# Attention and channel mix in one hand-ordered kernel: a new order of steps, filler matmuls ahead of the first sums, and two store queues for the last four tiles

## The chip, the cores and the metric

The kernel runs on one core of one Trainium2 chip. The metric is the device time of one execution, in microseconds. The core has TensorE (PE, with its weight loads listed as PEld), VectorE (DVE), ScalarE (ACT), GpSimd (POOL) and SyncE (SP). Each of them takes its own instructions strictly in the order of the program, apart from weight loads, which can be fetched ahead. ACT, POOL and SP also issue transfers.

## The reference, cut to what matters

There are 8 batches, 8 heads, 576 positions and 64 elements per head; `phi` has 32 memory slots per head.

```python
a = exp(phi - max(phi)); a = a / (sum(a) + 1e-9)
k_m = einsum('bhsm,bhsd->bhmd', a, k);  v_m = einsum('bhsm,bhsd->bhmd', a, v)
scores = q @ k_m.T / sqrt(64);  attn = softmax(scores)
x = (attn @ v_m), heads side by side: (8, 576, 512)
x_prev = x moved down by one position, zeros in front
xk = mu_k * x + (1 - mu_k) * x_prev;   xr = mu_r * x + (1 - mu_r) * x_prev
k2 = relu(xk @ w_k) ** 2               # 512 -> 1024
out = sigmoid(xr @ w_r) * (k2 @ w_v)   # (8, 576, 512)
```

## The kernel before, in words

**The order of the work.** Everything after the set-up is a list of short words, `PLAN` (lines 19 to 57). Lines 674 to 687 walk through it: the first time that a word such as `1:s` comes, the step starts and issues its instructions up to its first `yield`; the next time, it goes on from there. So `1:s 1:s 1:s` is the score matmuls of batch 1, then the exponentials of its first half of heads, then those of the second half. Words between two such parts are issued between them. Since each engine works in the order of issue, `PLAN` is the order of every engine's queue. `BANKS` (line 60) gives, in order of creation, which of the 8 PSUM banks each matmul result takes.

**The words.** `p:` words issue loads on POOL's queue (`preload`, line 165): `p:k:1` is k of batch 1, `p:wk:0-4` the first half of `w_k`'s columns. The loads of k, v, q and the weights turn f32 into bf16 on the way. k and v of a batch share one of two buffers, and so do q and phi, so batch 3 follows batch 1 in the same place. A word with a batch number is a step of that batch's attention:

- `exp` (L255, ACT) makes the exponentials of phi; `z` (L289, PE, and L293, DVE) sums them and takes the reciprocal `rz`; `kv`, `k`, `v`, `kg`, `vg` (L279, PE) are the sums over positions; `c00d` and the like (L262 ACT, L264 DVE) cast k of batch 0, which ACT's queue loads in f32 as `k0f`.
- `ak`, `nk` (L315 ACT, L317 DVE) scale `k_m` by `rz`; `tk` (L345 PE, L351 DVE) transposes it; `q0`, `q1` (L364, DVE) turn q; `s` (L377 PE, L385 ACT) gives scores and their exponentials `e`.
- The softmax sums of batches 1 to 7 are made on DVE: `fe` (L411), `fs` (L417, L418), `fo` (L423), then `w0`, `w1` (L430). For batch 0 they are made by PE and ACT: `l` (L393 PE, logarithm L401 ACT), `hNz` or `rNz` (L406 ACT, exp of the negative logarithm; `h` is one half of the positions of one half of the heads, `r` all positions), then `y` or `w` (L430 DVE).
- `x0`, `x1` (L336 PE, L444) are attention times values in two halves of the positions, copied out by ACT; `xv` gives half of the copies to DVE. `dd` (L456) takes the difference to the position before; `k0d`, `r2e` and the like (L467 or L469, then L471) make xk and xr: `d` scales on DVE, `e` on ACT, and DVE adds. Batch 0 has mixed weights instead: `mk`, `mr` (L336, `mxps`, PE) and `uk`, `ur` (L517; `a` on ACT, `d` on DVE).

Words with `c` are the first matrix of the channel mix: `c3:1s` is columns 128 to 255 of `w_k` for the fourth stretch of tokens (L603, PE), then relu and square. Without a letter the relu is on ACT (L611) and the square on DVE (L620); with `s` both are on ACT (L618); with `v` both are on DVE (L609, L620). Stretch 0 is batch 0 and has two halves, `a` of 320 and `b` of 256 positions; the later stretches are 512 tokens, the last 448. `g:5` (L636 PE, L640 ACT) is the gate of 128-token tile 5, `o:5` (L653 PE, L659 DVE) its second matrix and the product, followed by `store` (lines 579 to 591). The last tile, 35, is done in two parts of 384 and 128 columns.

**Filler.** `keep_busy` (line 215) issues matmuls on a tile of zeros whose result nobody reads (L219). `WARM` issues 78 of 64 columns at the start; `0:busy7_2` issues 7 of 512 columns, `0:busy1x4_5b` one of 4 x 64.

**The table.** `0:tb` (L252) loads ACT's second table of functions; the first holds the logarithm that batch 0 needs.

**The store.** A tile of 128 tokens goes out in two pieces of 64 rows:

```python
            eng.dma_start(out=dst, in_=o[p:p + n, cols])
            if t >= NTOK // 128 - 2:
                eng = nc.scalar
```

so the first piece is issued by SP, and for tiles 34 and 35 the second by ACT; for all others both by SP.

Of the kernel before, what the change touches and what calls it, by code (L numbers as in the profile page):

```python
# [16 lines left out]


PLAN = [
# [37 lines left out]
]  # L57

WARM = (78, 1)
BANKS = (  # L60
    "0123456701452370614523670145276301452763014263015762310476251642510764235174236501423601754214215672"
    "4165704136257413605237415327605247610524761052467354263452741023745102637405127405127651402751402635"
    "4026154026351407435071570267135426071354607132456071345601256013427501345041245142572431546417452046"
    "054720413207512"
)

PRE = "q:0g id:"
# [9 lines left out]
def kernel(  # L77
# [18 lines left out]
    NTOK = B * S  # L96
# [482 lines left out]
    def store(o, t, cols):  # L579
        g = t * 128  # L580
        eng = nc.sync
        while g < (t + 1) * 128:
            b, r = divmod(g, S)
            p = g - t * 128
            j, p0 = divmod(r, QR)
            n = min(QR - p0, (t + 1) * 128 - g)
            dst = out[b].rearrange("(p j) d -> p j d", j=NJ)[p0:p0 + n, j, cols]
            eng.dma_start(out=dst, in_=o[p:p + n, cols])
            if t >= NTOK // 128 - 2:
                eng = nc.scalar  # L590
            g += n

# [50 lines left out]
    def value(t, hs=((0, 1),), n=1):  # L643

        def go():
            p = t * 128 % (2 * S)
            for n_, (h0, h1) in enumerate(hs):
                if n_:
                    yield
                cols = slice(h0 * Dm // n, h1 * Dm // n)  # L650
                pv = ps_tile([128, Dm], F32, "pv")
                for fi in range(NF):
                    nc.tensor.matmul(pv[:, cols], lhsT=sq[:, fi, p:p + 128],  # L653
                                     rhs=wv_sb[:, fi, cols], start=(fi == 0), stop=(fi == NF - 1))
                yield
                if t not in outs:
                    outs[t] = work.tile([128, Dm], F32, name="o", tag="o", bufs=4)
                o = outs[t]
                nc.vector.scalar_tensor_tensor(o[:, cols], in0=gated[t][:, cols], scalar=1.0, in1=pv[:, cols],  # L659
                                               op0=AL.add, op1=AL.mult)  # L660
                store(o, t, cols)
        return go
# [55 lines left out]
```

## Time and profile before

| what | us |
|---|---|
| median of 3 runs | 203.02 |
| the runs | 202.95, 203.02, 203.92 |
| the profiled execution, its own time | 203.86 |
| its span, first to last instruction | 202.1 |
| what lies around the span | 1.76 |
| PE busy (94% of the span) | 190.5 |
| DVE busy (74%) | 149.8 |
| ACT busy (69%) | 139.6 |
| mean clock granted to PE, share of full speed | 0.983 |

A row of a timeline is start, duration, engine, line, operation, result<-operands, count, and in brackets how long the engine stood idle before it and what ended that. A row of grouped lines is line, engine, operation, shapes, count, busy time, mean duration of one in ns, then idle time before. A row of windows is the stretch, its length, busy time and count of PE, PEld, DVE, ACT and POOL, the granted clock, the busy share of the DMA engines (it can pass 1) and GB/s. The load rows give bytes and microseconds from issue to landing.

### The profile page before, as it was taken

To read this page: it belongs to the slowest core of one execution; us is meant where nothing else is said; L and a number is where in the kernel's file an instruction comes from. 1 tells how busy PE (TensorE), PEld (TensorE's weight loads), DVE (VectorE), ACT (ScalarE), POOL (GpSimd) and SP (SyncE) were. 2 spreads that over 40 slices of the span, in tenths; PEclk is the share of its full clock that TensorE was granted. 3 is DMA by queue.
4 is the path that set the end of the run, shared out by engine and by line. 5 is a ranking of instruction groups with operands and counts; after the bars stand their busy time and mean duration, and the time that the engine had idled before them with its cause. 6 is when DMAs were issued, how large, how long until landed. Compare 5 with 4: busy or idle time off the path is not lost.

```text
span 202.1 us, 5328 instructions
## 1 busy us (share of the span) xinstructions
PE 190.5 (94%) x2171; PEld 100.0 (49%) x2192; DVE 149.8 (74%) x314; ACT 139.6 (69%) x310; POOL 28.5 (14%) x43
## 2 busy tenths in 40 slices
PE   7399999999999999999999999999999999999990
PEld 7235665675554445444447854444444444444450
DVE  2136789889999999999998998999983804735241
ACT  2428668977887999997979989884486591446030
POOL 7544210511005400027000000000000000000000
PEclk9759999999999999999999999999999999999999
DMA  5999999999999999669999700122512200342455
GB/s 192 278 208 266 206 207 257 209 224 238 258 278 249 233 284 213 205 152 232 212 225 229 193 2 13 43 55 52 133 24 54 57 0 20 84 103 56 104 133 128
DMA packets 24521, 31.88 MB, mean 158 GB/s; under 512 B 1960, under 2 KB 19120, under 8 KB 24496
## 3 DMA queue, kind: packets, MB, share of 16 engines
q0 software_dynamic: 16848, 20.32, 53.2%
q1 hardware_dynamic: 6336, 9.18, 18.0%
q10 hardware_dynamic: 1312, 2.03, 3.0%
q8 instruction: 17, 0.28, 0.5%
q14 instruction: 8, 0.07, 0.1%
HBM read 38.28 MB, written 9.44 MB: 236 GB/s over the span
## 4 chain that ended last, share of the span: by engine, by line
PE 78%; DMA 11%; DVE 5%; ACT 2%; issue 1%; POOL 0%; ACTq 0%; DVEq 0%
PE pk L603 28%; PE pv L653 24%; PE pr L636 13%; DMA kv<-in_v_dram 8%; PE kvps L279 4%; PE idle L219 3%; DMA k0f<-in_k_dram 3%; PE scps L377 2%; PE nops L336 1%; DVE diff L456 1%; DVE xkT L471 1%; PE zps L289 1%; DVE se L417 1%; PE mxps L336 1%; PE ktps L345 1%
## 5 line engine op out<-in xcount | busy, mean ns | idle before, releaser
L603 PE MATMUL pk<-xkT,wk 128*128 128x512 bf16 (+4 forms) x342 | 68.1, 339 | 1.3 <-DVE xkT L471 0.3
L653 PE MATMUL pv<-wv,sq 128*128 128x512 bf16 (+3 forms) x322 | 66.4, 353 | 0.3
L603 PEld LDWEIGHTS <-wk 128*128 128x128 bf16 x352 | 32.8, 98 | 29.2 <-issue 2.5
L611 ACT ACTIVATE rl<-pk 128x512 bf16<-128x512 f32 (+3 forms) x63 | 34.8, 568 | 16.5 <-PE pk L603 8.6
L653 PEld LDWEIGHTS <-sq 128*128 128x128 bf16 x328 | 30.8, 98 | 29.7 <-ACT sq L618 0.4
L659 DVE SCALAR_TENSOR_TENSOR o<-sg,pv 128x512 f32<-128x512 f32 (+3 forms) x41 | 24.4, 612 | 22.9 <-PE pv L653 12.4
L636 PE MATMUL pr<-wr,xrT 128*128 128x512 bf16 x139 | 34.9, 379 | 0.3
L640 ACT ACTIVATE sg<-pr 128x512 f32<-128x512 f32 x36 | 21.2, 606 | 15.1 <-DVE o L659 7.6
L618 ACT ACTIVATE sq<-rl 128x512 bf16<-128x512 bf16 (+5 forms) x56 | 26.0, 502 | 0.7
L636 PEld LDWEIGHTS <-xrT 128*128 128x128 bf16 x144 | 13.8, 98 | 16.1 <-DVE xrT L471 0.3
L467 ACT ACTIVATE mu_d<-diff,mu 128x576 bf16<-128x576 bf16 x24 | 17.1, 771 | 4.0 <-DVE diff L457 3.7
L444 ACT CAST x<-nops 128x256 bf16<-128x256 f32 (+1 forms) x46 | 15.6, 435 | 5.1 <-PE nops L336 4.9
L620 DVE TENSOR_TENSOR sq<-rl 128x512 bf16<-128x512 bf16 (+5 forms) x48 | 14.7, 334 | 3.5 <-ACT rl L611 3.1
L430 DVE TENSOR_TENSOR atn<-e,lz 128x576 bf16<-128x576 bf16 (+2 forms) x18 | 11.8, 687 | 1.3 <-ACT lz L406 1.1
L219 PE MATMUL idle<-zeros 128*128 128x64 bf16 (+3 forms) x103 | 11.5, 282 | 1.0 <-DVE zeros L150 1.0
L609 DVE TENSOR_SCALAR rl<-pk 128x512 bf16<-128x512 f32 (+3 forms) x17 | 9.8, 580 | 3.5 <-PE pk L603 2.2
L364 DVE STREAM_TRANSPOSE qT<-q 128x576 uint32<-128x576 uint32 x16 | 11.9, 760 | 0.2 <-DMA q<-in_q_dram 0.2
L385 ACT ACTIVATE e<-scps 128x288 bf16<-128x288 f32 x32 | 10.5, 417 | 2.2 <-PE scps L377 2.2
L471 DVE TENSOR_TENSOR xrT<-x,mu_d 128x1152 bf16<-128x1152 bf16 x14 | 10.5, 749 | 1.0 <-ACT mu_d L467 0.9
L456 DVE TENSOR_TENSOR diff<-x 128x1024 bf16<-128x1024 bf16 (+1 forms) x21 | 10.4, 552 | 0.8 <-ACT x L444 0.4
L469 DVE TENSOR_SCALAR mu_d<-diff,mu 128x576 bf16<-128x576 bf16 x32 | 10.8, 378 | 0.3
L255 ACT ACTIVATE em<-ph 128x1152 bf16<-128x1152 f32 (+1 forms) x9 | 9.6, 1069 | 1.8 <-DMA ph<-in_phi_dram 1.8
(68 smaller groups left out, 150.8 us busy)
## 6 DMA issues: line engine op xcount, KB each, us to landing
out_dram<-o SPq DMA_DIRECT2D x61, 128.0 KB, 2.4
ph<-in_phi_dram POOLq DMA_DIRECT2D x7, 576.0 KB, 16.4
kv<-in_k_dram POOLq DMA_DIRECT2D x7, 576.0 KB, 16.8
q<-in_q_dram POOLq DMA_DIRECT2D x7, 576.0 KB, 17.6
kv<-in_v_dram POOLq DMA_DIRECT2D x7, 576.0 KB, 15.6
k0f<-in_k_dram ACTq DMA_DIRECT2D x2, 576.0 KB, 6.8
wk<-in_moe_w_k_dram POOLq DMA_DIRECT2D x2, 512.0 KB, 13.8
wv<-in_moe_w_v_dram POOLq DMA_DIRECT2D x2, 512.0 KB, 20.2
```

Of the source, the lines that this page charges most:

```text
L219: nc.tensor.matmul(ps.rearrange("p (a b) -> p a b", b=64), lhsT=zeros, rhs=zeros[:, :64].unsqueeze(1).to_broadcast([128, blocks, 64]), sta ...
L444: (nc.vector.tensor_copy if both and i > 1 else nc.scalar.copy)(st["x"][:, i, sl], pss[i])
L467: nc.scalar.activation(t[:, i], st["d"][:, pr + i, :], AF.Copy, scale=mu1[:, o:o + 1])
L471: nc.vector.tensor_add(dst, st["x"][:, pr:pr + n], t)
L603: nc.tensor.matmul(pk[:, p0 - lo:p1 - lo], lhsT=wk_sb[:, di, fi * 128:(fi + 1) * 128], rhs=xk_T[:, di, p0 % RING:p0 % RING + p1 - p0], sta ...
L611: nc.scalar.activation(rl, pk, AF.Relu, scale=HALF ** 0.5)
L618: nc.scalar.activation(sq[:, fi, p:p + p1 - p0], rl[:, part], AF.Square)
L620: nc.vector.tensor_mul(sq[:, fi, p:p + p1 - p0], rl[:, part], rl[:, part])
L636: nc.tensor.matmul(pr, lhsT=xr_T[:, di, c0:c0 + 128], rhs=wr_sb[:, di, :], start=(di == 0), stop=(di == ND - 1))
L640: nc.scalar.activation(gated[t], pr, AF.Tanh, scale=0.5)
L653: nc.tensor.matmul(pv[:, cols], lhsT=sq[:, fi, p:p + 128], rhs=wv_sb[:, fi, cols], start=(fi == 0), stop=(fi == NF - 1))
L659: nc.vector.scalar_tensor_tensor(o[:, cols], in0=gated[t][:, cols], scalar=1.0, in1=pv[:, cols], op0=AL.add, op1=AL.mult)
```

## The change

1. The list of steps is a new one. It has the same attention steps, matmuls, loads and stores; some steps change the engine of their copies, scalings, relus and squares. In batch 0 two of the four reciprocals and weighings are merged: `0:h0z 0:h1z 0:y0 0:y1` become `0:r0z 0:w0`.
2. At the head, after the 78 fillers, one filler of 256 and 13 of 512 columns are put in before the first `0:z`; the other fillers of the head are distributed differently, and three single ones come later (`0:busy1_5`, `0:busy1x5_3b`, `0:busy1x3_1b`). The second cast on DVE (`c10d`) and the turn of q (`0:q0`) now come before the reciprocal of `0:z`. The table load `0:tb` moves from the middle of stretch 0 to the place between `0:uk0d` and `0:uk0a`.
3. POOL's loads are in another order: `wk:4-8`, `wk:0-4`, `phi:1` instead of `wk:0-4`, `phi:1`, `wk:4-8`; then k1, q1, wr, v1, wv, phi2, wv, v2, k2, q2 as before; then q3, k3, phi3, v3 instead of v3, phi3, k3, q3; then phi4, phi5, q4, k4, v4, k5, v5, q5, phi7, v6, phi6, k6, q6, k7, v7, q7 instead of phi4, k4, v5, v4, phi5, q4, q5, k5, phi7, k7, phi6, v6, k6, q7, v7, q6.
4. For the last four tiles, not two, the second piece is issued by ACT.
5. `BANKS` is another string to match.

The head and the end of the list, the line with the sums of batch 3 (`3:kv`), the stretch from the scores of batch 7 to its last word that makes xk, and the store:

```diff
 PLAN = [
-    "p:q:0h 0:exp1 0:c00d 0:c01a 0:exp0 0:z 0:kg0 0:busy7_2 0:z 0:c11a 0:c10d 0:kg1 0:q0 0:busy1x3_1b 0:ak 0:tk",
-    "0:busy1x4_5b p:v:0g 0:q1 0:busy1x4_2b p:v:0h 0:busy1x5_3b 0:busy1x4_4b 0:tk 0:s1 0:s1 0:s0 0:s0 0:mub 0:mub",
-    "0:busy2_1 0:l2 0:l2 0:l3 0:l3 0:busy3_5 0:h3z 0:y3 0:h2z 0:y2 0:l0 0:l0 0:vg0 0:l1 0:l1 0:h1z 0:vg1 0:nm1",
-    "0:busy5_0 0:nm0 0:y1 0:h0z 0:y0 0:busy2_3 0:busy1_4 0:mk1 0:uk1d 0:uk1a p:wk:0-4 0:mk0 0:uk0a c0:2b 0:uk0d",
-    "c0:1av c0:1av c0:1av c0:2av p:phi:1 1:exp 0:mr0 0:ur0a 0:ur0d c0:2b c0:2b c0:3bv c0:1bv 0:mu c0:2av c0:2av 0:mu",
-    "c0:1bv p:wk:4-8 1:z c0:6av c0:7as c0:7as c0:5bv p:k:1 1:k 1:z 1:ak c0:6av c0:6av c0:7as c0:3bv c0:0bs c0:4bv",
...
-    "g:5 o:7 2:fe 2:fs 2:fo 2:w0 g:7 2:w1 2:xv0 o:7 3:z 3:z 2:xv0 2:xv0 3:kv 2:xv1 2:xv1 p:phi:4 o:4 p:k:4 3:ak 2:xv1",
...
-    "c5:7 6:fs 6:fo 6:w0 6:w1 g:18 g:18 5:r2e o:18 o:18 c5:4s c5:4s c5:4s 7:s 7:s 7:s 7:fe 5:r2e 7:fs g:19 g:21 g:21",
-    "c5:7 g:19 7:fo 7:w1 c5:1 c5:1 c5:1 6:x0 6:x0 7:w0 o:17 c5:3s o:17 6:x0 6:x1 6:x1 6:x1 6:dd 6:k2d 6:k2d o:19 g:20",
-    "g:20 g:26 o:20 o:20 6:k0d 7:x0 o:19 7:x0 7:x0 g:26 g:22 o:21 o:21 6:k0d g:24 7:x1 g:22 7:x1 7:x1 7:dd 7:k2d",
-    "7:k2d 7:k0e o:23 7:k0e c6:2s c6:0s c6:0s c6:0s g:23 g:23 c6:6v 6:r0d c6:1s 6:r0d c6:7v c6:7v 6:r2e 6:r2e c6:6v",
...
-    "c8:7s o:32 o:34 o:34 g:32 o:32 o:28 g:35 g:35 o:28 o:33 g:33 o:33 o:35 o:35 o:35 o:35",
+    "0:exp1 0:busy1x4_2b 0:busy13_9 0:c00d 0:c01a 0:c10d 0:exp0 0:z 0:kg0 0:c11a 0:q0 0:z p:q:0h 0:busy7_2 0:kg1",
+    "0:busy2_e0 0:busy1x4_e0b 0:q1 0:ak 0:tk 0:tk 0:busy1x6_5b 0:busy1x7_e1b 0:s0 0:s0 0:s1 0:s1 0:busy1x4_4b",
+    "0:busy1_4 0:mub 0:mub 0:l0 0:l0 0:l1 p:v:0g 0:vg0 0:l1 0:r0z 0:l3 0:l2 0:l2 0:h2z 0:w0 p:v:0h 0:vg1 0:nm1",
+    "0:busy2_3 0:nm0 0:y2 0:l3 0:h3z 0:y3 0:busy2_1 0:busy5_0 0:mk0 0:uk0d 0:tb 0:busy1_5 0:mk1 0:uk1d 0:uk0a 0:uk1a",
+    "p:wk:4-8 c0:7as c0:7as 0:mr0 0:ur0d p:wk:0-4 c0:4bv c0:4bv 0:ur0a 0:mr1 c0:1bv c0:1bv c0:1bv p:phi:1 c0:2bv",
+    "c0:7as c0:7bv c0:7bv c0:7bv 1:exp 0:ur1d c0:2a c0:2a p:k:1 1:z c0:4as c0:4as c0:4as c0:0as c0:0as c0:0as 1:k",
+    "p:q:1 0:busy1x5_3b c0:4bv c0:2a c0:5bs 1:z 0:busy1x3_1b 0:ur1a 1:nk 0:mu 1:tk 1:tk 1:q0 1:q1 c0:5bs c0:5bs",
...
+    "2:x1 2:x1 g:4 3:q0 o:5 g:4 3:z 2:xv0 2:xv0 o:7 p:v:3 3:kv 3:z 3:av 3:ak o:4 2:xv0 2:dd 2:k2e 2:k0d 3:tk 3:tk o:6",
...
+    "c5:0s o:16 c5:2 7:tk 4:r2e 7:s c5:4s 7:s 7:s 5:r2d c5:7s c5:7s c5:0s c5:6 6:fs 6:fo c5:0s o:17 o:17 o:19 4:r2e",
+    "g:18 g:18 g:21 7:fe g:21 5:r2d g:23 o:16 g:23 c5:3s c5:3s g:19 g:19 6:w0 6:w1 6:x0 c5:2 6:x0 6:x0 o:18 7:fs",
+    "c5:3s 7:fo 6:x1 7:w0 o:18 6:x1 7:w1 g:20 6:x1 6:dd o:21 o:21 g:22 g:20 g:22 7:xv1 7:xv1 7:xv1 6:k0d 6:k0d 6:k2d",
+    "6:k2d o:20 7:x0 7:x0 7:x0 7:dd o:20 o:22 o:19 c6:0 c6:5 c6:5 c6:5 c6:0 c6:1 7:k0d 7:k0d c6:0 g:26 g:26 c6:1 o:23",
+    "7:k2d 7:k2d c6:4v c6:2s c6:2s c6:2s o:22 c6:4v c6:4v 6:r0d c6:1 c7:6s c7:6s g:25 c6:7s 7:r0d 7:r0d c8:2 c6:7s",
...
+    "c8:6 c8:6 c8:6 c8:7v c8:7v c7:3 c7:3 c7:3 g:35 g:34 g:34 c8:1v o:30 c8:4 c8:4 o:28 g:28 g:28 o:28 g:30 g:30 o:30",
+    "o:31 o:31 c8:5 g:33 g:32 c8:4 c8:5 o:29 o:33 o:32 o:29 g:32 o:32 o:33 g:35 o:34 o:34 o:35 o:35 o:35 o:35",
 ]
...
-            if t >= NTOK // 128 - 2:
+            if t >= NTOK // 128 - 4:
                 eng = nc.scalar
```

More of the change, by code (lines that the diff above doesn't have):

```diff
@@ L60 @@
 BANKS = (
[L61 to L64, printed above, removed]
+    "0123456701263470521653247061507642314057623140576237234523724571043752643756142376145037615024374370"
+    "1431762401362457016253401672351406725406732540673254163720432701643706125437061543706154320761543015"
+    "4632154601546512670354267034127534120354703546713254671325671432546371546325016472506725075235210451"
+    "2674132764374635270"
 )
```

47 rows, old and new, of the table PLAN are left out of this document.

## The prediction

> **What bounds the kernel now.** I read the page first: busy shares and the granted clock by slices of 5 us.
>
> ```profile
> PE 190.5 (94%) x2171; PEld 100.0 (49%) x2192; DVE 149.8 (74%) x314; ACT 139.6 (69%) x310; POOL 28.5 (14%) x43
> PE   7399999999999999999999999999999999999990
> PEclk9759999999999999999999999999999999999999
> ```
>
> PE is busy nearly all the time, so the end moves only if PE starts its real work earlier, runs it faster, or the tail after the last matmul shrinks. All that is missing of PE and of its clock lies in the first three slices and the last. Windows of a fraction of a microsecond give the clock's edges (columns: length, busy PE, PEld, DVE, ACT, POOL, clock, DMA share, GB/s):
>
> ```profile
> 4.40:5.00 0.60, 0.42 (x15) 0.30 (x11) 0.00 (x0) 0.00 (x0) 0.60 (x2) 1.00 1.08 421
> 7.25:7.50 0.25, 0.00 (x0) 0.00 (x0) 0.13 (x1) 0.25 (x2) 0.25 (x1) 0.99 1.11 295
> 7.50:7.75 0.25, 0.00 (x0) 0.00 (x0) 0.00 (x0) 0.25 (x2) 0.24 (x1) 0.50 1.09 290
> 14.20:14.40 0.20, 0.20 (x3) 0.14 (x2) 0.17 (x1) 0.00 (x0) 0.00 (x0) 0.70 1.29 215
> ```
>
> The column of the clock has 1.00 from the start, but the matmuls tell more: 15 of the 78 fillers fit into 0.42 us at 4.4, where all 78 took 3.83, so full speed began at about 4.1. The clock falls to half at 7.50 and is back at about 14.3. The timeline shows what PE did around that:
>
> ```profile
> 0.99 3.83 PE L219 MATMUL idle<-zeros 128*128 128x64 bf16 x78 [0.99 <-DVE zeros L150]
> 6.92 0.67 ACT L262 CAST kv<-k0f 128x576 bf16<-128x576 f32 x1 [0.88 <-DMA k0f<-in_k_dram]
> 7.50 0.68 ACT L255 ACTIVATE em<-ph 128x576 bf16<-128x576 f32 x1
> 8.23 0.40 PE L289 MATMUL zps<-ones,em 128*128 128x2 bf16 x9 [3.41 <-ACT em L255]
> 9.16 3.17 PE L219 MATMUL idle<-zeros 128*128 128x512 bf16 x7
> 9.83 0.46 DVE L264 CAST kv<-k0f 128x576 bf16<-128x576 f32 x1 [0.99 <-DMA k0f<-in_k_dram]
> 9.83 0.67 ACT L262 CAST kv<-k0f 128x576 bf16<-128x576 f32 x1 [1.65 <-DMA k0f<-in_k_dram]
> 10.20 0.77 DVE L364 STREAM_TRANSPOSE qT<-q 128x576 uint32<-128x576 uint32 x1
> 12.26 0.67 PE L279 MATMUL kvps<-kv,em 64*32 64x64 bf16 x36
> 12.97 0.62 ACT L315 ACTIVATE kbd<-kvps,rz 128x128 bf16<-128x128 f32 x2 [2.47 <-PE kvps L279]
> 20.07 0.70 PE L336 MATMUL mxps<-atn,vmm 32*64 32x256 bf16 x40
> 22.95 0.48 PE L336 MATMUL mxps<-atn,vmm 32*64 32x320 bf16 x24
> ```
>
> PE idles 3.4 us for the exponentials, then fills with 7 matmuls at 0.45 us each. The second half of k was cast at 10.50, but its sum starts only at 12.26: the slow fillers stand in front. Everything of batch 0 follows from there, up to 20.07. At full clock a 512-column matmul costs 1.73 / 8 = 0.216 us (chain of waits):
>
> ```profile
> 163.37 1.73 PE pv L653 x8
> ```
>
> **The change part by part.**
>
> *Filler, clock and the head.* The new fillers start at 4.82 and last 0.11 + 13 x 0.216 = 2.9 us, to 7.7; a gap of 0.5 us is left, for ACT still casts k ahead of the second exponentials, so the sum of phi stays at 8.23. The clock fell after 2.7 us without matmuls; I take it that 0.5 us doesn't do it. Then 9 + 36 small matmuls and 7 fillers (1.51) end by 10.4, and the sum of k starts when its cast is done, at 10.55: **1.7 earlier**. The reciprocal now stands behind the second cast and the turn of q on DVE: 9.83 + 0.46 + 0.77 + 0.16 = 11.23, later than the sum's end at 11.0, so the scaling of k starts at 11.28 instead of 12.97 (1.69 earlier). Transposes and scores at full clock give back another 0.3 to 0.4. ACT's softmax chain then has the same length within 0.1 (two half reciprocals become one whole). So the mixing matmuls start at about 17.9 instead of 20.07.
>
> There ACT now loads its table first. It cost
>
> ```profile
> 33.40 1.28 ACT L252 ACT_TABLE_LOAD   x1
> ```
>
> in the middle of stretch 0, where PE hid it. Now ACT is free at 17.4, loads until 18.7 and casts until 19.6 the two blocks that the first key needs; without the load it would cast from 18.3. Price 0.4. The first key ends at 19.9 with `mr0` next. Before, `mr0` started at 22.95 with three keys done; the changed kernel is at that point after two more keys (0.99): 20.9. Less two fillers in later words (0.13 + 0.08): **1.9 us** at equal work.
>
> *Loads.* They don't move with PE. POOL's queue moves the same first loads, and each takes what it took:
>
> ```profile
> 9.86 0.75 POOL L140 DMA_DIRECT2D q<-in_q_dram  x1 [2.12 <-DMA q<-in_q_dram]
> q<-in_q_dram POOLq DMA_DIRECT2D x1, 576.0 KB, 17.6
> 30.29 0.92 PE L377 MATMUL scps<-qT,kmT 32*32 32x288 bf16 x32
> 37.92 0.77 POOL L140 DMA_DIRECT2D q<-in_q_dram  x1
> q<-in_q_dram POOLq DMA_DIRECT2D x1, 576.0 KB, 22.9
> 41.80 0.76 POOL L136 DMA_DIRECT2D ph<-in_phi_dram  x1 [3.11 <-ACT em L255]
> ph<-in_phi_dram POOLq DMA_DIRECT2D x1, 576.0 KB, 20.7
> 59.56 0.80 PE L279 MATMUL kvps<-kv,em 64*32 64x128 bf16 x72
> ```
>
> q of batch 1 lands at 27.46; two turns of 0.77 end at 29.0, so its scores end at 29.3 at the earliest. They ended at 31.2, at 0.1 less work done: a cap of 1.9 to 2.0. Batch 3 is tighter: q3 goes ahead of v3 now, so `3:kv` needs all four loads of batch 3, and the last of the same four landed at 37.92 + 22.9 = 60.8. Before, `3:kv` started at 59.56. The changed list has `o:5`, `2:x1` and `g:4` more ahead of it: 1.73 + 0.27 + 0.86 = 2.86. Cap: 59.56 + 2.86 - 60.8 = **1.6 us**. I take this cap, not 1.9. (Further on, k7 and v7 no longer hold up phi6, v6 and k6 behind them in POOL's queue; that relieves a stretch where PE hardly waited, so I count nothing.)
>
> *Steps in the middle.* The same matmuls, other engines for some copies. I count no new wait in the forecast; the range is 0.5 gained to 2.3 lost, by the third rival. Windows, columns as above:
>
> ```profile
> 60.00:80.00 20.00, 19.84 (x255) 9.50 (x247) 19.38 (x40) 17.69 (x44) 5.23 (x7) 1.00 1.18 249
> 80.00:100.00 20.00, 19.84 (x236) 9.28 (x237) 19.55 (x35) 18.72 (x41) 5.22 (x7) 1.00 0.90 201
> ```
>
> PE loses 0.16 in 20 us although DVE is 97% busy: the old order just fits.
>
> *Tail.* SP issues five pieces back to back; ACT has room.
>
> ```profile
> 195.71 3.16 SPq L588 DMA_DIRECT2D out_dram<-o  x5
> 196.87 0.75 DVE L659 SCALAR_TENSOR_TENSOR o<-sg,pv 128x384 f32<-128x384 f32 x2 [0.56 <-PE pv L653]
> 197.46 1.13 ACTq L588 DMA_DIRECT2D out_dram<-o  x2
> ```
>
> SP's last issue starts at 198.3, 0.63 after the one before; without the piece of tile 33 in front it starts about when ACT's second does, at 198.0: **0.3 us**. On ACT the second pieces of 32 and 33 wait for their products, and the gate of tile 35 is queued behind them; it is due about 3 us later, so nothing waits. Since the last four tiles now come closer together, the transfers could also crowd: 0.4 gained to 0.4 lost. The Trainium skill, "DMA: Bandwidth & Descriptors", section "Issuing engines are not separate DMA queues", says that issuing from several engines saves only the sequencer's time, usually small beside the transfer; by it the tail would give about nothing and the sum would be 202.2.
>
> **The sum.** Against the profiled execution's own 203.86 (span 202.1 and 1.76 around it): 1.6 + 0.3 = 1.9 gives **201.9**. The median of the runs shown is 203.02, 0.84 less than the profiled one; one run, 203.92, is like it. How long the clock stays low may differ between executions: the fall at 7.50 is 3.4 us after the rise at 4.1, and the return at 14.3 twice that after the fall. Had it come back one such step earlier, at 10.9, the last two or three of the seven fillers would have run fast and the sum of k would have started about 1 us earlier. I read the two faster runs so. The changed kernel has no low stretch left, so I don't take the 0.84 off: against the median the gain is 1.1, or 0.55%. If instead the profile adds the 0.84, the time is 201.1. The Trainium skill, "TensorE: Matmul & The Clock Gate", section "What's actually happening", has a free-running window of 3413 ns and one busy window to get the full clock; the two steps here agree with its length, but matmuls resumed at 8.23 and took 6 us, so a window not quite full did not count.
>
> **The rivals.** Half a per cent, 1.0 us, is about what a measurement of this kernel can tell from no change.
>
> 1. *The loads set the pace further* (same). v3 is issued last and shares the queue with the load behind it. If it lands only with that one, 1.7 us after 60.8 (phi4 landed at 41.80 + 20.7 = 62.5), the 1.6 is gone, 203.5; half of it gives **202.7**. For it: loads in one queue overlap, and the DMA share is still 1.18 from 60 to 80 us. Against: nothing makes the order of landings change.
> 2. *Filler does not hold the clock* (the change fails in what it says). Should the clock first rise at 7.5 and not at 4.1, six fillers run at 0.45 and the rest end at 9.1; the sum of k starts at 11.3, 0.75 later: **202.6**, and the same whenever the phase is bad. Against: here the 78 fillers did reach full speed before they ended.
> 3. *DVE becomes the bound around batch 7* (slower). From `7:s` to the last word that makes its xk the changed list has for DVE 2 `fs`, 2 `fo`, 1 `fe`, 4 `w`, 2 `dd`, 5 scalings of two, 6 additions, 6 products of `o`, 4 squares, 1 `xv`, where the old one had 1, 1, 1, 2, 2, 3, 4, 4, 2, 0:
>
> ```profile
> L423 DVE STREAM_TRANSPOSE lz<-se 128x1152 f32<-128x1152 f32 x7 | 9.6, 1372 | 0.1
> L417 DVE TENSOR_REDUCE se<-eT 128x36 f32<-128x1152 bf16 x7 | 9.5, 1351 | 0.2
> L469 DVE TENSOR_SCALAR mu_d<-diff,mu 128x576 bf16<-128x576 bf16 x32 | 10.8, 378 | 0.3
> L471 DVE TENSOR_TENSOR xrT<-x,mu_d 128x1152 bf16<-128x1152 bf16 x14 | 10.5, 749 | 1.0 <-ACT mu_d L467 0.9
> L430 DVE TENSOR_TENSOR atn<-e,lz 128x576 bf16<-128x576 bf16 x14 | 10.1, 754 | 0.2
> ```
>
> With these, and 0.68 for `o`, 0.41 for a square, 1.9 for `dd`, that is some 27.5 us for DVE; PE has 7 `o`, 7 `g`, 6 keys and small ones in the same stretch, 25.2. Before it was 18 against 22.6. If DVE comes to `7:s` with nothing done in advance, PE waits 2.3: **204.2**. It decides once DVE's lead is under those 2.3 us; `6:fs`, `6:fo` and others (about 6 us) don't depend on `7:s`, and DVE may have done them, which speaks against it.
>
> **How the numbers follow.** Forecast 201.9, chance 0.52 (its own spread 201.1 to 202.6; 0.44 of it below 202.0). Loads 0.24, mostly same. Clock 0.07, same. DVE 0.17, slower. Faster 0.47, same 0.35, slower 0.18. The range goes from 201.0 (no cap by loads and the tail's best) to 203.9 (between the loads' worst and DVE's).
>
> **What would show it.** Right: clock 1.00 from 4.1 on; the sum of k's second half at 10.5 to 10.6; `mxps` at 17.9; a wait for v3 before `3:kv` at 60.8; SP's last issue under 0.9 us after the last matmul. Wrong: PE idle for `xkT` or `atn` after 90 us; loads of batch 3 past 61; the clock at 0.5 after 8 us.

## The result and the profile after

The changed kernel takes 201.70 us (median of 5 runs, 201.34 to 201.81). The kernel before took 203.53 beside it (median of 5, 202.95 to 203.92). The ratio is 0.9911, with a 95% interval of 0.9885 to 0.9936: faster by 0.9%. The profiled execution has 201.34 and a span of 199.6; before it was 203.86 and 202.1. In experiment 2 below, three of the twelve executions are over 1.5% longer than its fastest and are left out of its ratio, and the only trace is of one of these three, at 205.52.

The page of the changed kernel, the same lines as before:

```profile
span 199.6 us, 5369 instructions
PE 191.9 (96%) x2187; PEld 100.7 (50%) x2207; DVE 151.8 (76%) x321; ACT 134.3 (67%) x301; POOL 28.7 (14%) x43
PE   8979999999999999999999999999999999999991
PEclk9999999999999999999999999999999999999998
```

The dent in the first slices, where PE stood still and the clock fell, is gone from both rows. The timeline of the head shows how:

```profile
0.99 6.70 PE L219 MATMUL idle<-zeros 128*128 128x64 bf16 x92 [0.99 <-DVE zeros L150]
7.72 0.38 PE L289 MATMUL zps<-ones,em 128*128 128x2 bf16 x9
8.03 0.45 PE L279 MATMUL kvps<-kv,em 64*32 64x64 bf16 x36
8.41 1.68 PE L219 MATMUL idle<-zeros 128*128 128x512 bf16 x7
10.57 0.67 ACT L262 CAST kv<-k0f 128x576 bf16<-128x576 f32 x1 [2.90 <-DMA k0f<-in_k_dram]
11.08 0.65 PE L279 MATMUL kvps<-kv,em 64*32 64x64 bf16 x36 [0.98 <-DVE kv L264]
18.23 0.85 PE L336 MATMUL mxps<-atn,vmm 32*64 32x320 bf16 x24
19.83 0.76 PE L603 MATMUL pk<-xkT,wk 128*128 128x320 bf16 x4
20.52 0.48 PE L336 MATMUL mxps<-atn,vmm 32*64 32x320 bf16 x24
```

The 14 fillers run on from the 78, and the 7 later ones take 1.68 us where they took 3.17. The first 36 small matmuls (8.03) take 0.45 where they took 0.67; the 0.65 of the second 36 (11.08) has a short pause in it. But k's second half is cast at 10.57, not at 9.83, and PE waits 0.98 for it. `mr0` starts at 20.52, before at 22.95, but with two keys (0.99 us of matmuls) less done and two fillers (0.21) still to come: 22.95 - 20.52 - 0.99 - 0.21 = **1.2 us** at equal work. From the chain of waits, around `3:kv`, and the last products with the issues beside them (timeline):

```profile
60.51 0.38 PE nops L336 x8
60.88 0.06 issue
60.95 0.92 PE kvps L279 x72
```

```profile
192.82 4.00 SPq L588 DMA_DIRECT2D out_dram<-o  x5
194.49 2.60 ACTq L588 DMA_DIRECT2D out_dram<-o  x3
195.13 0.75 DVE L659 SCALAR_TENSOR_TENSOR o<-sg,pv 128x384 f32<-128x384 f32 x2 [0.67 <-PE pv L653]
```

`3:kv` starts at 60.95; with the 2.86 us of work put ahead of it, the old pace would have had it at 62.42, so 1.47 is gained by there. The last products start at 195.13, before at 196.87: 1.74. From there to the end of the execution it is 201.34 - 195.13 = 6.21, before 203.86 - 196.87 = 6.99: another 0.78. Together 1.74 + 0.78 = 2.52, the whole difference of the two profiled executions (203.86 and 201.34).

### The profile page after: what moved, and what is told of

The parts are those of the page before. It is cut to its first block, busy times and chain, and to the rows that moved or that the text cites. A ratio compares the mean times of both kernels' runs of the same rounds, so it can differ in the third digit from the quotient of the medians.

```text
span 199.6 us, 5369 instructions
## 1 busy us (share of the span) xinstructions
PE 191.9 (96%) x2187; PEld 100.7 (50%) x2207; DVE 151.8 (76%) x321; ACT 134.3 (67%) x301; POOL 28.7 (14%) x43
## 4 chain that ended last, share of the span: by engine, by line
PE 87%; DMA 4%; DVE 3%; ACT 2%; issue 1%; ACTq 0%; DVEq 0%
PE pk L603 32%; PE pv L653 28%; PE pr L636 16%; DMA k0f<-in_k_dram 4%; PE kvps L279 3%; PE nops L336 2%; PE scps L377 2%; PE idle L219 2%; PE mxps L336 1%; DVE diff L456 1%; ACT mu_d L467 1%; ACT x L444 1%; PE zps L289 1%; PE ktps L345 1%; DVE o L659 0%
## 5 line engine op out<-in xcount | busy, mean ns | idle before, releaser
L603 PE MATMUL pk<-xkT,wk 128*128 128x512 bf16 (+4 forms) x343 | 67.3, 339 | 0.6 <-DVE xkT L471 0.2
L611 ACT ACTIVATE rl<-pk 128x512 bf16<-128x512 f32 (+3 forms) x65 | 35.7, 564 | 21.4 <-PE pk L603 16.2
L659 DVE SCALAR_TENSOR_TENSOR o<-sg,pv 128x512 f32<-128x512 f32 (+3 forms) x41 | 24.6, 615 | 19.8 <-ACT sg L640 13.2
L618 ACT ACTIVATE sq<-rl 128x512 bf16<-128x512 bf16 (+5 forms) x54 | 24.9, 497 | 0.8
L620 DVE TENSOR_TENSOR sq<-rl 128x512 bf16<-128x512 bf16 (+5 forms) x50 | 15.4, 340 | 3.9 <-ACT rl L611 3.5
L444 ACT CAST x<-nops 128x320 bf16<-128x320 f32 (+1 forms) x46 | 15.3, 423 | 2.9 <-PE nops L336 2.8
L219 PE MATMUL idle<-zeros 128*128 128x64 bf16 (+4 forms) x118 | 13.2, 274 | 1.0 <-DVE zeros L150 1.0
L469 DVE TENSOR_SCALAR mu_d<-diff,mu 128x576 bf16<-128x576 bf16 x42 | 13.9, 375 | 0.1
L467 ACT ACTIVATE mu_d<-diff,mu 128x576 bf16<-128x576 bf16 x14 | 10.2, 779 | 4.0 <-DVE diff L457 3.2
L471 DVE TENSOR_TENSOR xkT<-x,mu_d 128x1152 bf16<-128x1152 bf16 x14 | 10.4, 756 | 0.3
```

Of the source, the lines that this page charges most:

```text
L219: nc.tensor.matmul(ps.rearrange("p (a b) -> p a b", b=64), lhsT=zeros, rhs=zeros[:, :64].unsqueeze(1).to_broadcast([128, blocks, 64]), sta ...
L444: (nc.vector.tensor_copy if both and i > 1 else nc.scalar.copy)(st["x"][:, i, sl], pss[i])
L469: nc.vector.tensor_scalar_mul(t[:, i], st["d"][:, pr + i, :], mu1[:, o:o + 1])
L471: nc.vector.tensor_add(dst, st["x"][:, pr:pr + n], t)
L603: nc.tensor.matmul(pk[:, p0 - lo:p1 - lo], lhsT=wk_sb[:, di, fi * 128:(fi + 1) * 128], rhs=xk_T[:, di, p0 % RING:p0 % RING + p1 - p0], sta ...
L611: nc.scalar.activation(rl, pk, AF.Relu, scale=HALF ** 0.5)
```

## The experiments

Three groups of four, each on one chip beside runs of the kernel before (medians there 203.44, 203.31 and 203.44). Ratios are to those. The diffs show only the words of `PLAN` around a change, not whole lines; `BANKS` changes to match.

**1. The changed kernel without the new fillers.**

```diff
-0:exp1 0:busy1x4_2b 0:busy13_9 0:c00d
+0:exp1 0:c00d
```

> The changed kernel without the 14 new fillers ahead of the first z. Theory A (the fillers hold the clock, and that is most of the gain): PE idles from about 4.8 to 7.7, the granted clock falls to 0.5 somewhere between 7 and 10 us and is back by 11 to 14.5; the sum of k's second half comes at about 12 instead of 11.1; time 202.5 to 203.4, with a larger spread between executions than the changed kernel's 0.5 us. Theory B (the new order of the other steps gives the gain): 201.5 to 202.0.

202.78 (201.79 to 203.21), ratio 0.9959 (0.994 to 0.9977). That is theory A: the fillers are worth about 1.1 us in the new list. They also take the spread from 1.4 us (12 runs) to 0.5 (5 runs). Timeline:

```profile
8.29 0.40 PE L289 MATMUL zps<-ones,em 128*128 128x2 bf16 x9 [2.96 <-ACT em L255]
8.63 0.67 PE L279 MATMUL kvps<-kv,em 64*32 64x64 bf16 x36
9.89 0.67 ACT L262 CAST kv<-k0f 128x576 bf16<-128x576 f32 x1 [1.66 <-DMA k0f<-in_k_dram]
12.33 0.67 PE L279 MATMUL kvps<-kv,em 64*32 64x64 bf16 x36
```

The 36 small matmuls take 0.67, as in the kernel before, and not 0.45 as in the changed one at 8.03, and between the two rows the 7 fillers take 3.17 again: the clock is at half. (The column of the clock has 1.00 here all along; the durations say otherwise.)

**2. The kernel before with the 14 fillers alone.**

```diff
-0:exp1 0:c00d 0:c01a
+0:exp1 0:busy1x4_2b 0:busy13_9 0:c00d 0:c01a
```

> The kernel before with only the 14 fillers put in ahead of the first z, two PSUM banks named for them, nothing else changed. Theory A: clock 1.00 from 4 us on, sum of k's second half at 10.6 to 11.1 instead of 12.26, mixing matmuls about 1.5 us earlier, time 1.2 to 1.7 under the kernel before of the same chip (about 202.0), and the spread of the runs shrinks. Theory B: within 0.4 us of the kernel before.

204.92 (202.43 to 206.41), ratio 1.0036 (1.0003 to 1.0068): no gain at all, rather a loss, and a larger spread, so theory A fails. Yet the head does what it should: the sum of k's second half comes at 11.06, and `3:kv` 1.3 us earlier than before. By the starts of the products (L659) this lead of 1.3 lasts until 108 us of the kernel before, and from 124 on the new kernel is 1.65 behind; all that is lost is lost between them. The timeline at the sums of batches 6 and 7, and the windows around them:

```profile
111.06 2.06 PE L279 MATMUL kvps<-kv,em 64*32 64x128 bf16 x144 [1.90 <-DMA kv<-in_v_dram]
```

```profile
110.00:112.00 2.00, 0.94 (x80) 0.94 (x88) 0.68 (x1) 1.27 (x4) 0.00 (x0) 0.80 1.15 289
112.00:114.00 2.00, 2.00 (x94) 1.66 (x71) 1.79 (x5) 0.84 (x4) 0.00 (x0) 0.50 0.35 107
114.00:116.00 2.00, 2.00 (x17) 1.54 (x16) 1.93 (x6) 0.55 (x2) 0.00 (x0) 0.85 0.36 81
```

PE waits 1.90 us for v of batch 7 and then runs at half clock for about 3.4 us (an estimate from the three windows: 0.8 + 2.0 + 0.6). That is the trace of 205.52; what the shorter executions lost, no trace shows. The kernel before shows why PE waits, in its own chain of waits, in a stretch for which the prediction counted nothing:

```profile
93.81 16.76 DMA kv<-in_v_dram
110.57 0.04 issue
110.61 1.58 PE kvps L279 x144
```

There v7 lands at 110.57 and the sums start at 110.61. PE had come 0.1 us before. Whatever the head gained, PE would meet that load: with the earlier head it lands at 111.01, no earlier than before.

**3. and 4. The stores alone**: the changed kernel with the old limit (tiles 34 and 35), and the kernel before with the new one (tiles 32 to 35). The diff is that of experiment 3; experiment 4 has it the other way round.

```diff
-            if t >= NTOK // 128 - 4:
+            if t >= NTOK // 128 - 2:
```

> The changed kernel with the stores as before (only tiles 34 and 35 have their second piece on ACT's queue). Theory A, from SP's backlog: SP's last issue starts 0.3 us later after the last product, time 0.3 up, 202.0. Theory C (separate issuing engines change nothing, the transfers set the end): no change, 201.7. A third, from the two traces: what follows the last data was 0.5 us longer before (a fetch of instructions stood there); if the stores brought that on, 0.8 up.

202.06 (201.81 to 202.34), ratio 0.9932 (0.9911 to 0.9953).

> The kernel before with the second pieces of the last four tiles on ACT's queue and nothing else. Theory A: SP's last issue about 0.3 us earlier after the last product, time 0.3 less than the kernel before. Theory C: no change. If the fetch of instructions at the end hangs on the store code, 0.8 less.

203.27 (202.37 to 203.54), ratio 0.9986 (0.9969 to 1.0002). The medians are 0.36 above the changed kernel and 0.17 under the one before, which is at the limit of what they tell. The profiled executions tell it sharper, as time from the start of the last products to the end of the execution:

| | old stores | new stores |
|---|---|---|
| old list | 6.99 (before), 6.99, 6.87 | 6.68, 6.62 |
| new list | 6.60 | 6.21 (changed kernel), 6.19 to 6.24 in seven others |

From the left column to the right the stores change, from the upper row to the lower the list: the new stores give 0.2 to 0.4 in either list, the new list another 0.3 to 0.5. The stores' part fits SP's issues: its last one starts 1.45 us after the start of the last products before, and 1.14 in the changed kernel.

The list's part stands in the last instructions of POOL. Line 713 is where the profile puts the end of the program; its rows give engine, operation, count, shortest, median and longest in ns, and the first and last start in us. The kernel before, then the changed one:

```profile
L713 POOLq EVENT_SEMAPHORE  x4: 17/17/17, 200.8 to 202.0; - x4
```

```profile
L713 POOLq EVENT_SEMAPHORE  x4: 17/17/17, 198.8 to 199.5; - x4
```

POOL takes 1.2 us there before and 0.7 in the changed kernel. In all five traces of the old list it pauses once for 0.40 to 0.43 us between two of these instructions; in the nine of the new list no pause is over 0.07. SP's waits there, in the kernel before and in the changed one, are the same 0.4 to 0.5 longer:

```profile
SPq L713 <- PEq L713: 1.2, 2, 1.0
```

```profile
SPq L713 <- PEq L713: 0.7, 2, 0.5
```

The same five traces have a transfer of a queue of instructions at their very end, and the nine have none. The row of the DMA queues, from 199.5 us on in the kernel before:

```profile
q14 instruction: 1, 0.01, 0.4%
```

It is tempting to call this transfer the cause, but its time speaks against that. In the kernel before, the window from 201 to 202 us has no such row and the one from 202 to 203 has it: the transfer starts when POOL's and SP's last instructions (202.0) are done, after the pause; in all five traces it starts within 0.1 us behind SP's last instruction. So pause and transfer both go with the list of steps, and what makes POOL pause stays open.

The fourth experiment also shows the clock of the old head in another phase (windows):

```profile
8.00:8.50 0.50, 0.46 (x21) 0.45 (x25) 0.04 (x1) 0.00 (x0) 0.00 (x0) 0.77 1.14 297
11.50:12.00 0.50, 0.50 (x15) 0.10 (x16) 0.50 (x1) 0.00 (x0) 0.50 (x1) 0.81 1.24 224
```

From the means 0.77 and 0.81, the clock fell at about 8.27 and was back at about 11.69 (an estimate), and `mxps` started at 19.22 instead of 20.07: the same head, 0.85 earlier.

**5. The old list with the fillers of experiment 2 and one load moved.** k of batch 7 is issued behind k of batch 6.

```diff
-c3:6s c3:6s p:k:7 c3:7
+c3:6s c3:6s c3:7
...
-p:k:6 5:x1
+p:k:6 p:k:7 5:x1
```

> The old order of steps with the fourteen fillers (as in the run before, which had 204.92) and one load moved: k of batch 7 is issued behind k of batch 6 and no longer in front of phi, v and k of batch 6. Theory A (the filler's 1.2 us are lost because the last loads come too late: k7 waits 18.6 us on POOL for its buffer, and everything behind it lands late): the wait of 1.9 us for v7 at 111 goes, the clock stays full there, and the time is 202.0 to 202.5 with a spread under 0.7. Theory B (the old steps in the middle have no room for an earlier head, whatever the loads do): 203.5 to 205, with PE waiting at another place after 110. Theory C (the filler's gain is a matter of the clock's phase alone): about 203.4, as before.

202.40 (202.00 to 204.06), ratio 0.9962 (0.994 to 0.9983). By the two ratios that is 1.5 us less than without the move, by the medians of all executions 2.5. The wait at 111 is gone. POOL's timeline, first of the kernel of experiment 2, then of this one:

```profile
87.87 0.75 POOL L140 DMA_DIRECT2D kv<-in_k_dram  x1 [18.60 <-PE kvps L279]
89.08 0.76 POOL L136 DMA_DIRECT2D ph<-in_phi_dram  x1 [0.47 <-ACT kbd L315]
92.53 0.75 POOL L140 DMA_DIRECT2D kv<-in_v_dram  x1
```

```profile
79.85 0.76 POOL L136 DMA_DIRECT2D ph<-in_phi_dram  x1 [10.66 <-ACT em L255]
81.79 0.76 POOL L140 DMA_DIRECT2D kv<-in_k_dram  x1
87.82 0.74 POOL L140 DMA_DIRECT2D kv<-in_k_dram  x1 [5.28 <-PE kvps L279]
92.45 0.75 POOL L140 DMA_DIRECT2D kv<-in_v_dram  x1
```

v7 is issued at the same time in both. But when k7 waits 18.60 us in front, seven loads are issued between 87.9 and 93.3, and v7, the sixth of them, takes 18.5 us:

```profile
kv<-in_v_dram POOLq DMA_DIRECT2D x1, 576.0 KB, 18.5
```

```profile
kv<-in_v_dram POOLq DMA_DIRECT2D x1, 576.0 KB, 12.8
```

With phi6, v6 and k6 out from 79.9 on, it takes 12.8 and lands at 105.3, 3.8 us ahead of its sums (109.03). The move doesn't bring the late load forward; it takes its neighbours out of its way. Two of the 12 runs still took 203.8 and 204.1; there is no trace of one of them, and why stays open. The move without the fillers was not run, so what it is worth by itself is not known.

**6. The changed kernel with the old order of these loads** (phi6, v6, k6, q6 behind k7, and gone from their places before it).

```diff
-5:s 5:s 5:s p:k:7 c3:7s
+5:s 5:s 5:s p:k:7 p:phi:6 p:v:6 p:k:6 p:q:6 c3:7s
```

> The changed kernel, but phi, v, k and q of batch 6 are issued behind k of batch 7, at the place of k7, as the old order had it. Theory A: phi6, v6 and k6 are issued at about 87 to 91 instead of 78 to 86, v7 at about 91; PE waits for one of them at the sums of batches 6 and 7 (112.5 in the changed kernel), by 0.5 to 3 us, and the clock may fall after it: 202.5 to 205. Theory B (the order of the loads is worth nothing, as the prediction counted it): 201.7 within 0.3.

201.74 (201.51 to 201.82), ratio 0.9922 (0.9905 to 0.994): no loss, as theory B had it. Theory A, that the new order of loads is what lets the gain through, falls in this form. k7 waits 19.26 us on POOL again, and v7, issued at 90.79, takes 17.6 and lands at 108.4; but the new list has the sums of 6 and 7 later, at 112.6, behind more matmuls of other tiles. The changed kernel escapes twice: the loads are earlier (v7 lands at 106.2) and their reader is later (112.4). Either alone is enough: the first in experiment 5, the second here.

**7. The table load behind the keys of batch 0**, where the old list had it.

```diff
-0:uk0d 0:tb 0:busy1_5
+0:uk0d 0:busy1_5
...
-p:v:1 g:1 g:1
+p:v:1 0:tb g:1 g:1
```

> The changed kernel, but ACT loads the table of tanh only ahead of the first gate, behind the keys of batch 0, where the old order had it. Theory A (the head costs 0.4 by the table, but v3 and its neighbours, landing at 60.8, set the start of the sum of batch 3): the first keys come 0.3 to 0.6 earlier, PE waits longer in front of the sum of batch 3, which still starts at 60.8 to 60.9, and the end stays at 201.7 within 0.3. Theory B (what the head gains reaches the end): 201.2 to 201.4. Theory C (the 1.28 us hurt more in front of the gates): over 202.

202.26 (201.68 to 202.53), ratio 0.9944 (0.9925 to 0.9963). Longer, as theory C had it. The first key starts at 19.84, in the changed kernel at 19.83: the table load in the head costs nothing, and the 0.4 that I had put down for it was wrong. Behind the keys, in front of the gates, it does cost; this product started at 36.21 in the changed kernel, without a wait:

```profile
32.12 1.28 ACT L252 ACT_TABLE_LOAD   x1
37.01 0.53 PE L336 MATMUL nops<-atn,vb 32*64 32x320 bf16 x8 [0.72 <-ACT vb L326]
```

**8. A dose of work on DVE around batch 7.**

```diff
-6:x0 ... 6:x1 ... 7:x0
+6:xv0 ... 6:xv1 ... 7:xv0
```

> The changed kernel with three copies of batch 6 and 7's products out of PSUM moved from ACT to DVE (6:x0, 6:x1, 7:x0 become half DVE's), some 2 to 3 us more of DVE between 120 and 140. Theory A (DVE is 98% busy there and already sets the pace, as the third rival had it, only hidden): 2 us or more longer, 203.5 to 204.5, with PE waiting for xkT or atn. Theory B (DVE has a lead of some us over what PE needs from it): under 0.7 us longer, 201.7 to 202.4. Anything between measures the lead: the dose less the loss.

204.60 (204.33 to 204.82), ratio 1.0063 (1.0046 to 1.008): 2.9 us. DVE's busy time grew by 2.3 (154.1 against 151.8), and a copy now stands in its queue ahead of the softmax sums and waits for its products (DVE's timeline, then PE's):

```profile
133.38 0.89 DVE L444 CAST x<-nops 128x320 bf16<-128x320 f32 x2 [1.49 <-PE nops L336]
134.18 1.34 DVE L417 TENSOR_REDUCE se<-eT 128x36 f32<-128x1152 bf16 x1
```

```profile
139.80 0.64 PE L336 MATMUL nops<-atn,vb 32*64 32x256 bf16 x7 [0.73 <-DVE x L444]
```

That is theory A, a little above its range. 2.3 of work and 1.5 of waiting, 3.8 in all, cost 2.9, so by this estimate some 0.9 us fell into a lead that DVE had. It is a rough measure: at 139.80 PE waits for the copies themselves, and not for the xk or the weights behind them.

**9. The old list with three edits alone**: the fillers, k7 behind k6, the new stores (the diffs of 2, 5 and 4).

> The old order of steps with three edits alone: the fourteen fillers, k of batch 7 issued behind k of batch 6, and the second stores of four tiles by ScalarE's queue. Theory A (these three are nearly all of the gain; the steps placed anew add only the instruction fetch at the end of the program, which their runs lack and which costs about 0.4): 202.4 of the run without the new stores less 0.3 to 0.4, so 202.0 to 202.1, and from the last products to the end 6.5 to 6.7 us in the profiled execution with a fetch in the last 10 us. Theory B (the new steps carry more than that): 202.3 or more. Theory C (the new steps are worth nothing): 201.7.

201.99 (201.74 to 202.29), ratio 0.9926 (0.9907 to 0.9944), as theory A had it; 6.62 from the last products to the end, with POOL's pause of 0.4. The three edits give 1.45 us (203.44 to 201.99). The changed kernel has 0.29 less still, which is near the limit of what the runs tell, and the missing pause would account for that alone.

**10. Four scalings of batch 6 from DVE to ACT.**

```diff
-6:k0d 6:k0d ... 6:k2d 6:k2d
+6:k0e 6:k0e ... 6:k2e 6:k2e
```

> The changed kernel with the four scalings of batch 6's mixing for k moved from DVE to ACT, some 1.3 us less of DVE at 137 to 148. Theory A (DVE's lead in that stretch is small but above nothing: the dose of 2.4 us and a wait of 1.5 cost 2.9): relief changes nothing, 201.7 within 0.2. Theory B (PE is already held up by DVE there, a little at many places): 201.2 to 201.5. Theory C (the way over ACT is longer by 0.8 per pair and is late): over 202.

202.24 (202.07 to 202.48), ratio 0.9939 (0.9922 to 0.9956). Longer by 0.5, as theory C had it: the way over ACT is slower, and PE waits for it.

```profile
141.68 0.76 DVE L471 TENSOR_TENSOR xkT<-x,mu_d 128x1152 bf16<-128x1152 bf16 x1 [1.64 <-ACT mu_d L467]
```

```profile
143.82 2.32 PE L603 MATMUL pk<-xkT,wk 128*128 128x512 bf16 x10 [0.38 <-DVE xkT L471]
```

DVE did less and the kernel got longer, so it is not DVE's load that counts there, but when xk is ready. The second addition of xk ends some 1.06 later than in experiment 6, whose steps there are the changed kernel's (143.76 against 142.70), and the gate behind PE's keys starts 0.59 later (145.97 against 145.38): about 0.5 us of lead at that place.

**11. The changed kernel without the two late fillers.**

```diff
-p:q:1 0:busy1x5_3b c0:4bv
+p:q:1 c0:4bv
...
-1:z 0:busy1x3_1b 0:ur1a
+1:z 0:ur1a
```

> The changed kernel without the two late fillers around the sums of batch 1 (0.13 + 0.08 us of PE by the prediction). Theory A (PE has work ready there and the loads of batch 3, which landed at 60.8 with PE there at 60.9, allow no earlier start): the 0.2 shows at the first keys of batch 1 and is gone at 3:kv, 201.7 within 0.15. Theory B (it reaches the end): 201.5, the fastest so far.

201.56 (201.49 to 201.60, 4 runs), ratio 0.9903 (0.9885 to 0.9922). It is the lowest median, but inside the changed kernel's own runs (201.34 to 201.81), so not told from it. The trace has PE waiting 0.18 us for ACT's relu where the first filler stood, against 0.21 for both fillers: most of them covered a wait.

**12. A smaller dose on DVE.**

```diff
-7:x0 7:x0 7:x0
+7:xv0 7:xv0 7:xv0
```

> The changed kernel with the copies of batch 7's first products shared between ACT and DVE (7:x0 becomes half DVE's), about 1.6 us more of DVE at 142 to 147 and no new wait in DVE's queue. Theory A (DVE's lead over PE is about 1.0 us there, by the larger dose: 2.4 more work and 1.5 of waiting cost 2.9): 0.4 to 0.8 longer, 202.1 to 202.5. Theory B (the larger dose cost by its 1.5 us wait for the products alone, and DVE has a lead of 2 us or more): within 0.2 of 201.7. Theory C (no lead at all): 203.3.

201.70 (201.19 to 201.84), ratio 0.9905 (0.9887 to 0.9923). No loss. The dose was smaller than I had written: DVE's busy time rose from 151.8 to 152.6, by 0.8 and not 1.6: one pair of copies of 0.88. So this run only says that the lead is not under 0.8; that it isn't much longer is experiment 8's.

## Why the prediction was right, and where not

The forecast of 201.9 and the sign were right, but in part by luck: one cap was left unexamined, and edits of the list that had been counted as nothing took it away. The steps:

- *Filler and clock*: right. The clock stays full; without the fillers it falls (experiment 1). They are worth about 1.1 us. In the profiled execution no gap is left before the exponentials' sum (the fillers end at 7.69, the sum starts at 7.72); in experiment 5 the clock stayed full over one of 0.39. That the spread of the kernel before goes with the clock's return has two traces for it: experiment 4 caught a fall at about 8.27 and a return at about 11.69 in the old head. That step of 3.4 us agrees with the window of 3413 ns in the Trainium skill, "TensorE: Matmul & The Clock Gate", section "What's actually happening".
- *Head, 1.9 at equal work*: too much, 1.2. The sum of k's second half came at 11.08, not 10.55, since its load came 0.74 later. Without the fillers the load is not late; see the last section.
- *Table load, 0.4*: nothing in the head (experiment 7).
- *Cap by v3 at 60.8*: v3 was issued at 36.99 and took 23.8, so it landed at 60.8, to the tenth as predicted. PE came to `3:kv` at 60.88, so the cap stood right at PE but held up nothing; 1.47 was gained by there, for 1.6 forecast.
- *k7 and v7 off the queue, counted as nothing*: **this is the step that failed.** Without both that and the later place of the sums that read them, the gain of the head ends at 111 (experiments 2, 5, 6). I had worked out the cap by loads for batches 1 and 3 and not for batches 6 and 7, where the chain of waits shows a load landing 0.04 us before its reader starts. I took that as a stretch without waiting.
- *Steps in the middle, 0*: 0.27 gained from `3:kv` to the last products; PE's one wait of over 0.1 us there is 0.15, where before it had 0.12 and 0.16.
- *Tail, 0.3*: right, 0.2 to 0.4. By the rule quoted there from the Trainium skill, "DMA: Bandwidth & Descriptors", section "Issuing engines are not separate DMA queues", it would have been about nothing; here the time saved at the issuing queue shows at the end. The other 0.4 of the tail, POOL's pause, was not foreseen.
- *Rival 1* (loads later than 60.8) did not come, *rival 2* neither. *Rival 3* did not come, but it was nearer than I had put it: DVE's lead is about 0.5 us at one place (experiment 10), not under 0.8 at another (12) and roughly 0.9 by the larger dose (8), not some 6, and 2.3 us more work for DVE makes the kernel slower than before.

Against the profiled execution before, the sum was 1.9 and 2.52 was measured; the time came out near because the profiled execution after is the fastest of its kernel and the median lies 0.36 above it, and that too is luck. On medians it is 1.83 (203.53 to 201.70): 1.1 from the fillers, about 0.3 from the stores, and the rest of about the size of POOL's pause at the end.

## What to carry to other kernels

A gain at the head reaches the end only as far as every later load lets it: go through the loads in order, and for each compare the landing with the start of its reader, also where the profile shows no wait, for a load that lands 0.04 us before its reader is a cap already. In an in-order queue, a load that waits for its buffer holds back the loads behind it (18.6 us here), and these are then under way together with whatever is most urgent; so put the one that must wait last. Filler that keeps the clock up can pay even if it does no work (1.1 us here), but judge it in the whole kernel: alone, it paid nothing. And a row that goes with a delay is not yet its cause: compare the times of the two.

## What the runs showed of the hardware that was not expected

**Fillers move an instruction fetch.** k's second half was cast at 9.83, 9.89 and 9.99 us in the three kernels without the new fillers, and at 10.53 to 11.20 in the eleven with them, and the kernel before and that of experiment 2 differ in nothing else up to there. What goes with it is a transfer of a queue of instructions. The DMA queues of the changed kernel in the window from 8 to 9 us, and of the kernel before from 11 to 12, where it stands there:

```profile
q8 instruction: 1, 0.02, 6.1%
```

```profile
q8 instruction: 1, 0.02, 6.1%
```

6.1% of 16 engines for 1 us is one DMA engine for 0.98 us. It may be that with 14 matmuls more at the start PE comes earlier to the point where its next instructions are fetched; the fetch then falls among the last pieces of k. The place of the fetch is shown in all fourteen kernels (8 to 9 against 11 to 12); whose instructions it brings, and that it is what delays k, is inferred from its size and that company.

**The end of the program** can differ by 0.4 us: POOL pauses 0.40 to 0.43 us there or not at all (experiments 3 and 4). Which of the two went with the list of steps in all fourteen kernels, not with the stores. A fetch goes with it, but it starts after the pause.

**The clock falls in mid-kernel too.** A single wait of 1.9 us at 111 (the trace of experiment 2) was followed by 2 us at 0.50 and some slower time around them, so that the wait cost more than itself: the sums began 2.0 us later than in the kernel of experiment 5 (111.06 against 109.03), and the last products came 3.2 later (198.53 against 195.31).
